# Batch 0's keys turned in pairs of tokens, in another order with scores and products, and an earlier load of batch 1's values

## The chip, the cores and the metric

The kernel runs on one core of a Trainium2 chip. A core has a matrix engine (TensorE, PE in the profile, with its weight loads as PEld), VectorE (DVE), ScalarE (ACT), GpSimd (POOL) and SyncE (SP); the last two issue most of the transfers. Matrix products land in PSUM, eight banks of 128 partitions by 2 KB. The metric is device microseconds of one execution.

## The reference

There are 4 batches, 8 heads, 768 tokens and 64 features a head. The first part is attention whose keys and values are mixed between blocks of 96 tokens by a matrix P (8 x 8 a head), made doubly stochastic by five rounds; the second is an MLP over tokens and channels.

```python
for _ in range(5):
    P = exp(P - max); P = P / sum over -1; P = P / sum over -2
k_sorted = einsum('bhij,bhjcd->bhicd', P, k_b)     # v_sorted likewise
scores = scale * q_b @ k_sb^T                      # within a block of 96
attn = softmax(scores);  x = attn @ v_sb           # -> (4, 768, 512)
u = x + lam * (w_tok @ (alpha1 * x + beta1))
out = u + lam * (relu((alpha2 * u + beta2) @ w_ch1) @ w_ch2)
```

## The kernel before

Every engine works off its instructions in the order in which the program gives them (the `Engine` wrapper pins it). The framework puts in the waits, and hands out the buffers: PSUM is cut into two slots of two banks (`psa`) and four slots of one bank (`psb`), and a tile that needs a slot waits until all readers of the one before are done. In SBUF the tag `raw` has two buffers, shared by `k8` and `v8` (keys and values of batch 0), by the permuted second half of the token weights, and by the keys and values of the later batches.

Batch 0 is done apart from the others, with an order written out by hand (lines 900 to 1013). A "group" `g` is a pair of heads; there are four. The steps that matter here:

- `v_sort`, `v_mm`, `v_out` (lines 171, 393, 408) reorder, mix and store the values of batch 0 into `Vs`.
- `k_turn(0, g, psb)` (line 387, through `turn_slab`, line 238) mixes the keys of a group and turns them so that features lie on partitions. It takes one token at a time: for each of 12 tokens and both heads the 64 x 64 piece of `k8` is the stationary operand and `bigK` the moving one. Output half `t // 6` goes to one of two psB banks, on the 64 partitions of its head. `k_copy` (line 390) copies one bank, 128 partitions of 384 elements, into `KT0`, the keys that the scores read; one bank goes to VectorE (`copy`), the other to ScalarE (`act.copy`).
- `score(0, g, hf, ps)` (line 414) makes the scores of four blocks of a group and their exponentials on ScalarE, in one piece where the slot is `psa` and in two where it is two `psb` slots. With `fillers` it runs idle matmuls first.
- `pv_first(g)` (line 464) multiplies them with `Vs` (24 matmuls or so), and VectorE divides by the sums (`rc`, `x`).
- `wtok` turns the token weights, `first_mm(g)` is the first token product, `first_turn` turns x; then the units of the channel MLP (`h_unit`, `ch_unit`) follow, with the steps of the next batch put between them by the table `at` (`put`, lines 993 to 1071).
- `prep_scales` (line 272) is two short multiplications on VectorE. `scale_weights(g)` (line 793) scales a quarter of `W2p` on VectorE.
- `load_kv(b)` (line 195) issues the loads of the values and the keys of batch b from GpSimd's queue, each in two halves; `mix_v(1, n)` and `mix_k(1, n)` use them, `q_turn_late` the queries that `load_q(1)` brings.

In the order before, the keys of groups 0 and 1 are turned among the value products, then all four scores of these groups follow, then `pv_first(0)`, then the keys of groups 2 and 3:

```python
    score(0, 0, 0, psa)
    score(0, 0, 1, psa)
    score(0, 1, 0, psb, 1)
    score(0, 1, 1, psb)
    ...
    pv_first(0)
    kp2 = k_turn(0, 2, psb)
    kp3 = k_turn(0, 3, psb)
```

GpSimd's queue issues, in this order, the weights `W1p` and `W2p` (four blocks each, with the permutation of the token weights between them), then the values and keys of batch 1 and its queries.

Of the kernel before, what the change touches and what calls it, by code (L numbers as in the profile page):

```python
# [7 lines left out]
FT = mybir.dt.float32  # L8
# [8 lines left out]
def kernel(  # L17
# [31 lines left out]
    HB = BLK // 2  # L49
# [23 lines left out]
    pe = Engine(nc.tensor)  # L73
    dve = Engine(nc.vector)
    act = Engine(nc.scalar)
# [11 lines left out]
    def psa(shape, dtype, name):  # L87
        return pools["psA"].tile(shape, dtype, name=name, tag="psA")

    def psb(shape, dtype, name):  # L90
        return pools["psB"].tile(shape, dtype, name=name, tag="psB")

    def const(shape, dtype, name):
        return wts.tile(shape, dtype, name=name, tag=name)

    wz = const([128, 512], F16, "wz")
# [13 lines left out]
    KT0 = att.tile([128, H4, NB, 128], F16, name="kT0", tag="tw", bufs=2)  # L110
# [3 lines left out]
    k8 = att.tile([128, H4, 12 * D], F16, name="k8", tag="raw", bufs=2)  # L114
# [7 lines left out]
    def load_halves(dst, src):  # L122
        for th in range(2):
            pool.dma_start(
                dst[th * 64:(th + 1) * 64, :, :],
                src.rearrange("h (j th t) d -> th (h j) t d", j=NB, th=2)[th],
            )
# [64 lines left out]
                qn_of[b][:, kt, :, :], q[b, :, kt * 128:(kt + 1) * 128, :].rearrange("h p d -> p h d"),  # L192
            )

    def load_kv(b):
        for kv, src in ((1, v), (0, k)):
            raw = att.tile([128, HB, D], F16, name="raw", tag="raw", bufs=2)
            load_halves(raw, src[b])
            raw_of[(b, kv)] = raw
# [38 lines left out]
    def turn_slab(src, rhs, g, name, ps):  # L238
        if ps is psa:
            ps = ps([128, 2, 512], FT, name)  # L240
            ps = [ps[:, a, 0:384] for a in range(2)]
        else:
            ps = [ps([128, 384], FT, name)[:] for a in range(2)]
        for s in range(12):
            for h2 in range(2):
                t = (s + 6 * h2) % 12
                r = slice(h2 * 64, h2 * 64 + 64)
                pe.matmul(
                    ps[t // 6][r, (t % 6) * 64:(t % 6) * 64 + 64],
                    src[r, g, t * D:(t + 1) * D], rhs(r, g), start=True, stop=True,  # L250
                )
        return ps
# [19 lines left out]
    def prep_scales():  # L272
        dve.tensor_tensor(
            ab2col[:, 3 * CT:4 * CT], ab2col[:, 2 * CT:3 * CT], ab2col[:, 3 * CT:4 * CT], ALU.mult
        )
        dve.tensor_tensor(ab2col[:, 4 * CT:5 * CT], ab2col[:, 0:CT], ab2col[:, 3 * CT:4 * CT], ALU.mult)
# [44 lines left out]
    bigK = {}  # L321
# [65 lines left out]
    def k_turn(b, g, ps):  # L387
        return turn_slab(k8, lambda r, g: bigK[b][r, g, :], g, "k_ps", ps)

    def k_copy(b, g, ps, half, eng):  # L390
        eng(
            KT0[:, g, :, :].rearrange("p i (th u) -> p (i th) u", th=2)[:, :, 0:HB].rearrange(
                "p x (c t) -> p x c t", t=12
            )[:, :, :, half * 6:half * 6 + 6],
            ps[half].rearrange("p (t x c) -> p x c t", t=6, c=4),
        )

    def v_mm(b, n, out_):
        for s in range(8):
            for th in range(2):  # L400
                d = (s + 4 * th) % 8
                r = slice(th * 64, th * 64 + 64)
                pe.matmul(
                    out_[r, d * 64:d * 64 + 64], VD[r, n * 8 + d, :],
                    bigV[b][r, :, :].rearrange("p h i -> p (h i)"), start=True, stop=True,
                )

    def v_out(n, w, src, eng):
        eng(Vs[:, :, n * 8:(n + w) * 8], src.rearrange("p (d x) -> p x d", x=64))
# [4 lines left out]
    def score(b, g, hf, ps, fillers=0):  # L414
        if ps is psb:
            ps = [ps([128, 4 * BLK], FT, "sc_ps") for _ in range(2)]
            bank = [t_[:] for t_ in ps]
        else:
            ps = [ps([128, 2, 512], FT, "sc_ps")]
            bank = [ps[0][:, a, :] for a in range(2)]  # L420
        for _ in range(fillers):
            z = wz[:].bitcast(FT)[:, 0:192]
            pe.matmul(
                bank[0][:, 0:384], z[:, 0:128], z.unsqueeze(1).to_broadcast([128, 2, 192]), start=True, stop=True,
            )
        n = 128 if b == 0 else BLK
        keys = kT_of[b][:].rearrange("p g i t -> p (g i t)")
        for ii in range(4):
            i = 4 * hf + ii
            lo = (g * NB + i) * n  # L430
            w = min(128, H4 * NB * n - lo)
            for h2 in range(2):
                r = slice(h2 * 64, h2 * 64 + 64)
                pe.matmul(
                    bank[h2][0:w, ii * BLK:(ii + 1) * BLK], keys[r, lo:lo + w],
                    qT_of[b][r, g, i * BLK:(i + 1) * BLK], start=True, stop=True,
                )
        tag, bufs = ("ost", 4) if (b, g) == (0, 3) else ("et", 6)
        et = att.tile([128, 2, 4, BLK], F16, name="et", tag=tag, bufs=bufs)
        if len(ps) == 1:  # L440
            act.activation(
                et[0:n].rearrange("p a i t -> p a (i t)"), ps[0][0:n, :, 0:4 * BLK], AF.Exp, scale=scale
            )
        else:
            for a in range(2):
                act.activation(
                    et[0:n, a].rearrange("p i t -> p (i t)"), ps[a][0:n, :], AF.Exp, scale=scale
                )
        ets[(b, g, hf)] = et
# [11 lines left out]
        dve.tensor_tensor(dst, x_of[b][rows, kts, c], al, ALU.mult)  # L461
        dve.tensor_tensor(dst, dst, be, ALU.add)

    def pv_first(g):
        if g == 0:
            x_of[0] = moep.tile([128, 8, C], F16, name="x128", tag="x128", bufs=1)
        ps = psa([128, 2, 512], FT, "x_ps")[:, :, 0:480].rearrange("p a (k d) -> p a k d", d=80)
        for i in range(NB):
            for h2 in range(2):
                et = ets[(0, g, i // 4)][:].rearrange("p a i t -> p (a i t)")  # L470
                lo = (4 * h2 + i % 4) * BLK
                w = min(128, 8 * BLK - lo)
                val = Vs[:, (2 * g + h2) * NB + i, 0:D + 1]
                if i < 6:
                    pe.matmul(ps[0:w, h2, i, 0:D + 1], et[:, lo:lo + w], val, start=True, stop=True)
                else:
                    for a in range(3):
                        pe.matmul(
                            ps[96:128, h2, 3 * (i - 6) + a, 0:D + 1], et[:, lo + a * 32:lo + (a + 1) * 32], val,
                            start=True, stop=True,  # L480
                        )
        rc = att.tile([128, 2, 6], FT, name="rc", tag="rc", bufs=3)
        dve.reciprocal(rc[:], ps[:, :, :, D])
        dve.tensor_tensor(
            x_of[0][:, 0:NT, g * 128:(g + 1) * 128].rearrange("p k (a d) -> p k a d", a=2),
            ps[:, :, :, 0:D].rearrange("p a k d -> p k a d"),
            rc[:].rearrange("p a k -> p k a").unsqueeze(3).to_broadcast([128, NT, 2, D]), ALU.mult,
        )
# [406 lines left out]
    copy = dve.tensor_copy  # L895
# [24 lines left out]
    v_mm(0, 5, v5)  # L920
    v_mm(0, 2, v12[:, 512:1024])
    v_out(0, 1, v0, copy)
    kp0 = k_turn(0, 0, psb)
    v_out(6, 2, v67, copy)
    v4 = bank("v_ps")
    v_mm(0, 4, v4)
    v3 = bank("v_ps")
    v_mm(0, 3, v3)
    v_out(5, 1, v5, act.copy)
    k_copy(0, 0, kp0, 0, copy)  # L930
    k_copy(0, 0, kp0, 1, act.copy)
    kp1 = k_turn(0, 1, psb)
    v_out(4, 1, v4, copy)
    v_out(1, 1, v12[:, 0:512], act.copy)
    v_out(3, 1, v3, copy)
    v_out(2, 1, v12[:, 512:1024], act.copy)
    k_copy(0, 1, kp1, 0, copy)
    k_copy(0, 1, kp1, 1, act.copy)
    score(0, 0, 0, psa)
    score(0, 0, 1, psa)  # L940
    score(0, 1, 0, psb, 1)
    score(0, 1, 1, psb)
    prep_scales()
    pool.tensor_tensor(brow[0:1, :], bet1[:], lam1[:], ALU.mult)
    for j in range(1, 4):
        sp.dma_start(brow[32 * j:32 * j + 1, :], brow[0:1, :])
# [7 lines left out]
        pool.dma_start(W1p[:, :, g * 512:(g + 1) * 512], w1v[:, :, g * 512:(g + 1) * 512])  # L954
    permute(1, pool.tensor_copy, 0, 6)
    for g in range(4):
        pool.dma_start(W2p[:, g * 4:(g + 1) * 4, :], w2v[:, g * 4:(g + 1) * 4, :])
    moe_start(0)
    a1_of[0] = moep.tile([128, 8, C], F16, name="a1", tag="a1", bufs=1)
    pv_first(0)  # L960
    kp2 = k_turn(0, 2, psb)
    kp3 = k_turn(0, 3, psb)
    for g, kp in ((2, kp2), (3, kp3)):
        k_copy(0, g, kp, 0, copy)
        k_copy(0, g, kp, 1, act.copy)
    score(0, 2, 0, psa)
    score(0, 2, 1, psb)
    pv_first(1)
    score(0, 3, 0, psb)
    score(0, 3, 1, psa)  # L970
    for ks in range(4):
        wtok(ks, copy)
    wtok(4, act.copy)
# [10 lines left out]
    first_turn(2, psa)  # L984
    scale_affine(betaB)

    load_kv(1)
    load_q(1)
    pool.memset(Vs[0:BLK, :, D:GRP], 1.0)

# [23 lines left out]
    for b in range(1, B):  # L1014
        p = b - 1
# [42 lines left out]
        put(b, 0, "h", 4, lambda b=b: moe_cross(b, 1))  # L1058
        put(b, 0, "c", 2, lambda b=b: moe_affine(b, 1))

    for g, m in enumerate((10, 11, 12, 12)):
        put(0, 0, "h", m, lambda g=g: scale_weights(g))
    for n, at_ in enumerate(((0, 1, "c", 4),) * 3 + ((0, 1, "c", 5),) * 3 + ((0, 1, "c", 6),) * 2):
        put(*at_, lambda n=n: block_weights(n))
# [68 lines left out]
```

## Time and profile before

| | |
|---|---|
| median of 3 runs | 258.17 us (256.55 to 260.22) |
| profiled execution, its own time | 256.33 us |
| its span | 254.6 us |
| TensorE busy | 244.0 us (96%), mean granted clock 0.993 |
| VectorE, ScalarE, GpSimd busy | 174.1, 155.7, 46.1 us |
| moved by DMA | 31.09 MB, mean 122 GB/s |

The profile is of one execution. Times in it count from the first instruction, and the span ends with the last. Nearly every instruction carries line 65, the line of the wrapper, so that groups are told apart by the tiles they write and read: `k_ps` are the turned keys in PSUM and `kT` the copy of them, `sc_ps` scores, `et` their exponentials, `x_ps` the attention products, `wtok_ps` token weights, `tok_ps` token products, `raw` the loads of later batches. A chain of waits follows the work that ended last backwards, from each instruction to what released it. A table of windows gives the busy time of each engine in stretches of the span, then the granted clock of TensorE, the share of the DMA engines and GB/s.

### The profile page before, as it was taken

Reading aid. Unit: us, or ns where it says so; the run is one execution under the profiler, and the core shown is the slowest. Engines: PE = TensorE matmul, PEld = TensorE weight load, DVE = VectorE, ACT = ScalarE, POOL = GpSimd, SP = SyncE. Lnnn points to the kernel's source line nnn. Section 1 sums busy time; section 2 is a strip of 40 time slices with the busy share of each in tenths; the row PEclk is TensorE's granted clock in tenths of the full one; section 3 lists DMA queues with packets and bytes.
Section 4 is the critical chain, followed back from the end, with each engine's and each line's share of the span. In section 5 each row is a group of like instructions: output and inputs, shape, how many; then the busy total and the mean of one; then the engine's idle time right before and its main releaser. Section 6 shows DMA issues by size and latency. Waiting matters only on the chain.

```text
span 254.6 us, 6059 instructions
## 1 busy us (share of the span) xinstructions
PE 244.0 (96%) x2416; PEld 159.7 (63%) x2416; DVE 174.1 (68%) x461; ACT 155.7 (61%) x285; POOL 46.1 (18%) x70
## 2 busy tenths in 40 slices
PE   7897999999999999999999999999999999999994
PEld 2475765555465545556765797558756875686783
DVE  5884588667379868279896685398978862462773
ACT  4796675567788679786564696878364005837400
POOL 8699604000082010191000010000000000000000
PEclk9997999999999999999999999999999999999999
DMA  5999999998999997999961179710203132111023
GB/s 98 202 210 192 207 205 210 216 179 197 165 179 180 131 209 124 178 159 164 136 161 39 31 189 127 141 23 0 85 0 66 50 115 45 21 41 44 0 85 82
DMA packets 61936, 31.09 MB, mean 122 GB/s; under 512 B 50562, under 2 KB 57618, under 8 KB 61908
## 3 DMA queue, kind: packets, MB, share of 16 engines
q0 software_dynamic: 20976, 16.91, 45.7%
q1 hardware_dynamic: 40836, 13.76, 32.0%
q8 instruction: 19, 0.31, 0.5%
q14 instruction: 9, 0.07, 0.1%
q10 hardware_dynamic: 96, 0.03, 0.1%
HBM read 32.79 MB, written 8.65 MB: 163 GB/s over the span
## 4 chain that ended last, share of the span: by engine, by line
PE 77%; DVE 9%; ACT 6%; DMA 3%; issue 2%; POOL 1%; DVEq 0%; ACTq 0%; POOLq 0%
PE h_ps L65 28%; PE tok_ps L65 12%; PE px L65 8%; PE ch_ps L65 8%; PE pz L65 6%; PE py L65 5%; DMA v<-in_v_dram 3%; PE x_ps L65 3%; DVE x L65 3%; PE sc_ps L65 2%; DVE sums L65 2%; PE kmix_ps L65 2%; PE mix_ps L65 2%; ACT kT L65 1%; ACT vd L65 1%
## 5 line engine op out<-in xcount | busy, mean ns | idle before, releaser
L65 PE MATMUL h_ps<-a2T,W1p 128*128 128x384 bf16 x512 | 93.4, 326 | 0.3 <-DVE a2T L65 0.3
L65 PEld LDWEIGHTS <-W1p 128*128 128x128 bf16 x512 | 47.8, 98 | 30.7
L65 ACT ACTIVATE hTa<-h_ps 128x384 f16<-128x384 f32 x64 | 31.2, 490 | 30.6 <-PE h_ps L65 29.5
L65 ACT ACTIVATE hTb<-h_ps 128x384 f16<-128x384 f32 x64 | 31.3, 489 | 8.7 <-PE h_ps L65 8.7
L65 DVE SCALAR_TENSOR_TENSOR u<-tok_ps,x 128x512 f32<-128x512 f32 x21 | 14.5, 692 | 27.0 <-PE tok_ps L65 27.0
L65 PE MATMUL tok_ps<-a,w_tokT 128*128 128x512 f16 x126 | 30.3, 379 | 0.0
L65 ACT CAST kT<-kmix_ps 64x512 f16<-64x512 f32 x36 | 25.7, 713 | 7.0 <-PE kmix_ps L65 6.5
L65 ACT ACTIVATE et<-sc_ps 96x768 f16<-96x768 f32 (+2 forms) x36 | 24.6, 736 | 2.4 <-PE sc_ps L65 2.4
L65 ACT CAST u<-u 128x512 f16<-128x512 f32 x21 | 13.0, 618 | 20.4 <-DVE u L65 20.4
L65 PEld LDWEIGHTS <-sums 128*128 128x128 f16 x216 | 21.1, 98 | 3.8 <-issue 0.7
L65 PEld LDWEIGHTS <-hTa 128*128 128x128 f16 x192 | 18.2, 98 | 6.6
L65 PEld LDWEIGHTS <-hTb 128*128 128x128 f16 x200 | 18.5, 98 | 6.1
L65 PEld LDWEIGHTS <-w_tokT 128*128 128x128 f16 x126 | 12.3, 98 | 13.1 <-DVE a L65 0.3
L65 DVE TENSOR_TENSOR x<-x_ps,rcb 96x512 f16<-96x512 f32 x24 | 16.5, 687 | 0.8
L65 DVE TENSOR_TENSOR sums<-hTa,hTb 128x512 f16<-128x512 f16 (+2 forms) x27 | 8.9, 330 | 10.3 <-ACT hTb L65 10.0
L65 PEld LDWEIGHTS <-et 96*128 96x128 f16 (+4 forms) x288 | 12.6, 103 | 2.7
L65 DVE SCALAR_TENSOR_TENSOR ost<-px,u 128x256 f32<-128x256 f32 x27 | 11.3, 419 | 3.4 <-PE px L65 3.4
L65 PE MATMUL x_ps<-Vs,et 96*128 96x65 f16 (+4 forms) x288 | 13.5, 199 | 0.0
L65 PE MATMUL ch_ps<-W2p,hTa 128*128 128x512 f16 x48 | 11.9, 380 | 0.0
L65 PE MATMUL ch_ps<-W2p,hTb 128*128 128x512 f16 x48 | 11.7, 379 | 0.0
L65 POOL DMA_DIRECT2D qn<-in_q_dram x12 | 10.7, 915 | 5.2 <-DMA raw<-in_v_dram 4.8
L65 PE MATMUL sc_ps<-qT,kT 64*128 64x96 f16 (+1 forms) x256 | 10.0, 210 | 1.5 <-DVE x L65 0.7
(140 smaller groups left out, 351.2 us busy)
## 6 DMA issues: line engine op xcount, KB each, us to landing
out_dram<-ost SPq DMA_DIRECT2D x23, 192.0 KB, 2.4
raw<-in_v_dram POOLq DMA_DIRECT2D x6, 384.0 KB, 8.4
raw<-in_k_dram POOLq DMA_DIRECT2D x6, 384.0 KB, 10.8
Vs<-vscr SPq DMA_DIRECT2D x3, 768.0 KB, 7.9
W1p<-in_moe_w_ch_dram POOLq DMA_DIRECT2D x4, 512.0 KB, 11.6
W2p<-in_moe_w_ch_dram POOLq DMA_DIRECT2D x4, 512.0 KB, 15.6
qn<-in_q_dram POOLq DMA_DIRECT2D x12, 128.0 KB, 11.1
vscr<-mixed POOLq DMA_DIRECT2D x4, 384.0 KB, 5.0
```

The costliest lines, as they stand in the source:

```text
L65: ins = getattr(self.eng, name)(*args, **kwargs)
```

## The change

The keys of batch 0 are turned two tokens at a time: a 64 x 128 piece of `k8` is stationary, 12 matmuls a group in place of 24, and a head has a bank of its own, with the even tokens on its lower 64 partitions and the odd ones on the upper. A bank is copied in two pieces of 64 partitions, which write every second token. The keys of group 2 are now turned ahead of `pv_first(0)`, the scores of group 1 and the keys of group 3 follow behind it; `pv_first(0)` starts with one idle matmul; both banks of group 3 are copied by VectorE; some scores change between `psa` and `psb`; `prep_scales` comes later. The values of batch 1 are issued ahead of the last block of `W2p`, and the scaling of that block moves from unit 12 to unit 15 of the first half.

```diff
-    def load_kv(b):
-        for kv, src in ((1, v), (0, k)):
+    def load_kv(b, *kvs):
+        for kv in kvs or (1, 0):
+            src = (k, v)[kv]
...
+    def k_turn_pairs(g):
+        ps = [psb([128, 384], FT, "k_ps")[:] for a in range(2)]
+        for tp in range(6):
+            for h2 in range(2):
+                r = slice(h2 * 64, h2 * 64 + 64)
+                pe.matmul(
+                    ps[h2][:, tp * 64:tp * 64 + 64], k8[r, g, tp * 128:(tp + 1) * 128], bigK[0][r, g, :],
+                    start=True, stop=True,
+                )
+        return ps
+
+    def k_copy_pairs(g, ps, h2, eng):
+        dst = KT0[h2 * 64:h2 * 64 + 64, g, :, :].rearrange("p i (th u) -> p (i th) u", th=2)[:, :, 0:HB].rearrange(
+            "p x (c t) -> p x c t", t=12
+        )
+        for par in range(2):
+            eng(
+                dst[:, :, :, par::2],
+                ps[h2][par * 64:par * 64 + 64, :].rearrange("p (t x c) -> p x c t", t=6, c=4),
+            )
...
-    def pv_first(g):
+    def pv_first(g, fillers=0):
...
+        z = wz[:].bitcast(FT)[:, 0:240]
+        for _ in range(fillers):
+            pe.matmul(ps[:, 0, :], z[:, 0:128], z.unsqueeze(1).to_broadcast([128, 2, 240]), start=True, stop=True)
...
-    kp0 = k_turn(0, 0, psb)
+    kp0 = k_turn_pairs(0)
...
-    k_copy(0, 0, kp0, 0, copy)
-    k_copy(0, 0, kp0, 1, act.copy)
-    kp1 = k_turn(0, 1, psb)
+    k_copy_pairs(0, kp0, 0, copy)
+    k_copy_pairs(0, kp0, 1, act.copy)
+    kp1 = k_turn_pairs(1)
...
-    k_copy(0, 1, kp1, 0, copy)
-    k_copy(0, 1, kp1, 1, act.copy)
     score(0, 0, 0, psa)
     score(0, 0, 1, psa)
-    score(0, 1, 0, psb, 1)
-    score(0, 1, 1, psb)
-    prep_scales()
+    k_copy_pairs(1, kp1, 0, copy)
+    k_copy_pairs(1, kp1, 1, act.copy)
+    kp2 = k_turn_pairs(2)
+    k_copy_pairs(2, kp2, 0, copy)
...
     for g in range(4):
+        if g == 3:
+            load_kv(1, 1)
         pool.dma_start(W2p[:, g * 4:(g + 1) * 4, :], w2v[:, g * 4:(g + 1) * 4, :])
...
-    pv_first(0)
-    kp2 = k_turn(0, 2, psb)
-    kp3 = k_turn(0, 3, psb)
-    for g, kp in ((2, kp2), (3, kp3)):
-        k_copy(0, g, kp, 0, copy)
-        k_copy(0, g, kp, 1, act.copy)
+    pv_first(0, 1)
+    score(0, 1, 0, psa)
+    k_copy_pairs(2, kp2, 1, act.copy)
+    kp3 = k_turn_pairs(3)
+    k_copy_pairs(3, kp3, 0, copy)
+    k_copy_pairs(3, kp3, 1, copy)
+    prep_scales()
+    score(0, 1, 1, psb)
     score(0, 2, 0, psa)
-    score(0, 2, 1, psb)
+    score(0, 2, 1, psa)
     pv_first(1)
-    score(0, 3, 0, psb)
-    score(0, 3, 1, psa)
+    score(0, 3, 0, psa)
+    score(0, 3, 1, psb)
...
-    load_kv(1)
+    load_kv(1, 0)
...
-    for g, m in enumerate((10, 11, 12, 12)):
+    for g, m in enumerate((10, 11, 12, 15)):
         put(0, 0, "h", m, lambda g=g: scale_weights(g))
```

More of the change, by code (lines that the diff above doesn't have):

```diff
@@ L462, in first_affine @@
         dve.tensor_tensor(dst, dst, be, ALU.add)
-    def pv_first(g):
+    def pv_first(g, fillers=0):
         if g == 0:
             x_of[0] = moep.tile([128, 8, C], F16, name="x128", tag="x128", bufs=1)
-        ps = psa([128, 2, 512], FT, "x_ps")[:, :, 0:480].rearrange("p a (k d) -> p a k d", d=80)
+        ps = psa([128, 2, 512], FT, "x_ps")[:, :, 0:480]
+        z = wz[:].bitcast(FT)[:, 0:240]
+        for _ in range(fillers):
+            pe.matmul(ps[:, 0, :], z[:, 0:128], z.unsqueeze(1).to_broadcast([128, 2, 240]), start=True, stop=True)
+        ps = ps.rearrange("p a (k d) -> p a k d", d=80)
         for i in range(NB):
```

## The prediction

> **What bounds the kernel now.** I read the page's engine line and the 40 slices first, then the chain of waits in its early part, then a table of windows, the rows of the key copies, and the transfers.
>
> ```profile
> PE 244.0 (96%) x2416; PEld 159.7 (63%) x2416; DVE 174.1 (68%) x461; ACT 155.7 (61%) x285; POOL 46.1 (18%) x70
> ...
> PE   7897999999999999999999999999999999999994
> ...
> PEclk9997999999999999999999999999999999999999
> DMA  5999999998999997999961179710203132111023
> ```
>
> From slice 5 on (each is 6.4 us) TensorE is never below nine tenths: from about 41 us it only works off its list, so what the front loses or gains there is passed on to the end one for one. The DMA line says that the transfers fill the engines until about 58 us. So there are two things to follow: the front on the engines, and the arrivals. The chain of waits in the front:
>
> ```profile
> 16.96 0.39 ACT kT L65
> 17.35 2.96 ACT et L65 x6
> 20.31 0.91 issue
> 21.22 0.59 PE k_ps L65 x23
> 21.81 0.02 issue
> 21.83 0.57 DVE kT L65
> 22.40 0.14 issue
> 22.54 0.63 PE sc_ps L65 x16
> 23.16 1.57 PE x_ps L65 x24
> ```
>
> ScalarE is the bound up to 20.3 us, from 12 us on by the same chain (value copies, key copies, six exponentials of the scores of groups 0 and 1). Then TensorE, which had begun the keys of group 2 at 19.53, stands until 21.22: their psB banks are held by the scores of group 1. That wait is 1.48 us long in the list of waits. What it leaves behind is seen in windows cut to the clock's own steps:
>
> ```profile
> 15.97:19.39 3.42, 3.34 (x90) 2.41 (x83) 2.17 (x6) 3.42 (x9) 3.02 (x6) 1.00 1.16 211
> 19.39:22.80 3.41, 1.56 (x68) 1.31 (x66) 2.16 (x4) 1.77 (x5) 3.41 (x4) 1.00 1.20 165
> 22.80:26.21 3.41, 3.41 (x60) 2.94 (x54) 1.46 (x4) 2.59 (x6) 3.41 (x5) 0.50 1.16 220
> ```
>
> The second number is TensorE's busy time and the third from the right its granted clock. After a window with 1.56 us of work in 3.41 us (46%) the clock is half for the next one; the emptiest window before it that was not followed by this had 83%. In the half window the 24 products of `pv_first(1)` take 1.64 us, against 1.02 us for `pv_first(0)`.
>
> **The change, part by part.** The times below are of the span of the profiled execution (254.6 us; its own time is 256.33 us).
>
> *The turn.* 96 matmuls become 48. 24 of them took 0.55 us; sixteen score products, the nearest form with 64 rows and 128 columns, took 0.51 to 0.59 us, so twelve should take some 0.4 us. That is 0.1 to 0.2 us a group, on an engine that waits for banks and copies here. I take nothing; with no wait left it would be a gain of at most 0.8 us. One page of the Trainium skill speaks against it: "TensorEngine Tiling (Array Packing)", section "Tiling Modes", says that changing the tiling mode drains the engine, and the value products (64 by 64) now alternate with key turns of 64 by 128. Here a key turn of 64 by 64 runs from 16.03 to 16.84 us and the 64 by 128 scores behind it start at 16.77, inside it, so I count no drain; by the rule it would be one matmul's 0.19 us at each of some three added switches.
>
> *The copies.* Each bank now needs two copies of 64 partitions in place of one of 128. Four copies on VectorE become ten, four on ScalarE become six. The rows:
>
> ```profile
> L65 ACT CAST kT<-k_ps x4: 477/482/483, 15.5 to 22.2; 128x384 f16<-128x384 f32 x4
> L65 DVE CAST kT<-k_ps x4: 548/548/559, 15.7 to 22.3; 128x384 f16<-128x384 f32 x4
> ...
> 57.48 1.42 ACT L65 CAST kT<-kmix_ps 64x512 f16<-64x512 f32 x2 [2.45 <-PE kmix_ps L65]
> ```
>
> Back to back what counts is the distance of starts: 0.37 us on ScalarE (15.50 to 15.87) and 0.47 us on VectorE. The new copy is not in the trace. Low end on ScalarE: 0.37 us, as for 128 partitions. High end: 0.71 us, that of the later batches' key copies, two of which take 1.42 us. These also take 64 partitions and write every second element, but move 512 elements; by 384/512 that is 0.53 us, and I take it as the nearest in form. On VectorE I take 0.47, with 0.67 us (the same ratio of 0.53 to 0.37) as the high end.
>
> *The new order on ScalarE.* Starts: keys of group 0 at 15.50; value copies at 16.56 and 17.04 (0.48 each); exponentials of group 0 at 17.52 and 18.22 (0.70 each, 17.25 to 17.95 before); keys of group 1 at 18.92 and 19.45, done at 20.05. TensorE: `pv_first(0)` gets its psA slot when the first exponential is done (18.34), runs the added filler (two of 384 columns took 0.91 us, so about 0.5 us for 480) and 24 products in 1.02 us: about 19.9 us against 19.60. Only now come the scores (0,1,0), at 20.1, because the keys of group 1 end on ScalarE at 20.05; their exponential starts at 20.5. Then the second bank of group 2's keys, 21.2 to 22.3. The scores (0,1,1) want psB banks, and one of the four is held until that copy ends (or until VectorE's copies of group 3 at about 22.2): they start at 22.35. So the wait of 1.48 us isn't removed; TensorE stands from about 20.85 (end of the turn of group 3) to 22.35, 1.5 us, now behind key copies on ScalarE. Queued behind it on TensorE are (0,2,0), (0,2,1) and `pv_first(1)`, and ScalarE idles 0.5 us at each of two round trips. Exponentials of (0,1,1) 22.75 to 23.5, of (0,2,0) to 24.2, of (0,2,1) to 24.9. `pv_first(1)` needs the psA slot of (0,2,0), free at 24.3, because both scores of group 2 now sit in psA: it runs from 24.35 to 25.37 us at full clock, to 25.99 at half. Before it ended at 24.73.
>
> *To the first token product.* VectorE then does the reciprocal and the division (0.27 and 0.92 us) and five token-weight copies (1.47 us, 25.95 to 27.43), and the last matmul of `first_mm(0)` adds about 0.35: 25.37 + 0.03 + 0.27 + 0.92 + 1.47 + 0.35 = 28.4 us at full clock, 29.0 at half. Before it ended at 28.09. So the front loses 0.3 or 0.9 us. TensorE's work in 19.39 to 22.80 by this order is about 1.6 us of 3.41, near the 1.56 that was followed by the half clock, but where the windows fall differs from run to run. I take +0.5. Bounds: three pairs of key copies lie on this path, so 0.37 gives 3 x 2 x 0.16 = 0.96 less (-0.7) and 0.71 gives 1.08 more (+1.4 at full, +2.0 at half clock). The slower VectorE copy is hidden: group 3 would end at 23.9, and its scores start past 25.
>
> The Trainium skill, "TensorE: Matmul & The Clock Gate", section "Why this matters for your kernels", puts the drop of the clock at idle gaps of some 3 us. This trace differs: the longest gap before the half clock is 1.5 us. By the page no half clock would come here and the loss would be 0.3.
>
> *Small moves.* `prep_scales` (0.35 us on VectorE) goes from 17.83 to about 23.1, where VectorE has nothing until 25.4; its first reader is at 28.12 on ScalarE. `scale_weights(3)` (1.22 us) goes from unit 12 to unit 15, but is VectorE work that ran at 53.87 anyway, for matmuls at about 56. Both nothing.
>
> *The values of batch 1.*
>
> ```profile
> 25.72 2.96 POOL L65 DMA_DIRECT2D W2p<-in_moe_w_ch_dram  x4
> 28.95 0.54 POOL L65 DMA_DIRECT2D raw<-in_v_dram  x1 [0.26 <-PE x_ps L65]
> 31.21 0.53 POOL L65 DMA_DIRECT2D raw<-in_v_dram  x1 [1.72 <-DMA W1p<-in_moe_w_ch_dram]
> ```
>
> The second half is issued at 31.21 and lands 18.7 us later, at 49.9; the first `mix_v` starts at 50.78, so 0.9 us are to spare. The queue works in order and 512 KB take about 2.5 us, so with the last W2p block behind it the values land at 47.4 and that block at 49.9, where it is wanted at 53.87. W2p's last issue moves behind GpSimd's wait at 29 to 31 us (an issue waits until the eighth before it has landed: W1p's second block, 19.17 + 11.8 = 31.0). Behind it stand only the keys of batch 1, which waited until 40.76 anyway. The buffer that the values need is k8's, free after the turn of group 3 (20.85), and GpSimd comes there at 27.9. In the profiled execution this is worth nothing. In the median run it may be: that is 1.84 us longer than the profiled one. If late transfers are the whole of it, they are 2.74 us late; the next arrivals have 2.5 us (queries, 41.77 + 13.9 = 55.7 against 58.23) and 3.3 us (keys, 53.6 against 56.83), so 0.2 us is paid in place of 1.84: a gain of 1.6. If none of it is, zero. I take 0.8.
>
> **Sum.** 258.17 + 0.5 - 0.8 = 257.9; against the profiled execution's 256.33 it is +0.5, 256.8.
>
> **Rivals.** (1) *The front gets shorter.* The new copy costs ScalarE 0.37 and the clock stays full: -0.7. For it: half as many elements in all per copy. Against it: the later batches' copies. With the 0.8 of the loads 256.7, with 1.6 255.9; I give 256.3. (2) *Slower: the new wait on ScalarE.* The copy costs 0.71, TensorE stands 2 us before (0,1,1), and the half clock falls on `pv_first(1)`: +2.0, and no gain of the loads: 260.2. It decides as soon as a pair of copies takes over 1.2 us and the work in that window is near 46%. For it: all these copies sit on the engine that bounds the front. (3) *The earlier load isn't earlier*, because its buffer or its queue place isn't free: +0.5 and no gain, 258.7; the times 20.85 and 27.9 speak against it.
>
> **How the numbers follow.** Forecast 0.50 (its own range 256.3 to 259.2), rival 1 0.22, rival 2 0.20, rival 3 0.08. 255.9 and 260.2 are the ends of the unknown costs; as the runs of before lie from 256.55 to 260.22 about their median, I add about 1 below and 0.6 above: 254.8 to 260.8. 2% of the median, about what a measurement of this kernel can tell from no change, is 5.2 us. No case reaches that by itself: faster needs under 253.0, rival 1 and lucky runs (0.09); slower over 263.3, rival 2 and unlucky ones (0.08).
>
> **What would show it.** Right: the key copies of 64 partitions on ScalarE about 0.53 us apart; TensorE idle about 1.5 us ahead of the scores (0,1,1), released by ScalarE's kT; `first_mm(0)` done between 28.2 and 29.0; the values of batch 1 landed by 48 us; the slices after 41 us alike. Wrong: `pv_first(1)` done before 24.7, `first_mm(0)` before 27.8, a wait at `mix_v` or ahead of the last W2p block, or a time outside 254.8 to 260.8.

## The result and the profile after

The changed kernel takes 261.0 us (median of 6 runs, 260.66 to 262.30); the kernel before took 257.44 beside it (6 runs, 256.55 to 260.22): a loss of 3.6 us, where 257.9 us was forecast. The ratio on record is 1.0166 with a 95% interval of 1.0134 to 1.0199 (the two medians alone would give 1.0138). Two later sets of runs with the same kernel gave 259.63 (1.0098, 1.0054 to 1.0141) and 261.20 (1.0147, 1.0098 to 1.0195); single executions lie from 259.1 to 262.4, with one at 264.2. So the loss is 2 to 3.6 us by the medians, slower in each of the three intervals, but inside the 2% that counts as no change here.

The profiled execution took 262.3 us, its span 260.5. Its engine line, TensorE's slices and the granted clock:

```profile
PE 247.5 (95%) x2368; PEld 161.3 (62%) x2368; DVE 177.4 (68%) x467; ACT 157.8 (61%) x285; POOL 46.1 (18%) x70
...
PE   7966799999999999999999999999999999999994
...
PEclk9997589999999999999999999999999999999999
```

Slices 3 to 5 (13 to 33 us) have got emptier, slices 5 and 6 slower; from slice 7 on the digits are those of before. The chain of waits of the same execution, in the front:

```profile
20.02 3.19 PE x_ps L65 x26
...
24.50 0.57 ACT kT L65
...
25.72 0.35 PE sc_ps L65 x7
26.07 1.57 ACT et L65 x3
...
27.69 1.61 PE x_ps L65 x24
29.30 0.45 PE sc_ps L65 x8
...
29.78 1.20 ACT et L65 x2
...
31.02 1.44 PE wtok_ps L65 x12
32.46 1.77 PE tok_ps L65 x6
```

Before, one run of exponentials led to one run of TensorE. Now TensorE and ScalarE take turns: two idle and 24 real products (26 in the first row), scores, key copy, scores, exponentials, `pv_first(1)`, scores, exponentials, and only then the last token weights. `first_mm(0)` ends at 34.23 in place of 28.09.

Not all of these 6.1 us need belong to the change. The first value copies on ScalarE start at 11.99 in the profile of before and at 13.35 here, and between 11.9 and 13.7 in all profiles, whatever the kernel (13.31 with the loads alone, e4 below). The changed kernel's third profile (run e18 below, the fastest of its six executions) starts them at 11.93, so it stands beside before without that shift: `first_mm(0)` ends at 30.78 and the span is 257.3, both 2.7 us more than before. The rest of the span after `first_mm(0)` is 226.5 us in before, 226.3 here and 226.5 there. In these profiles the whole loss is in the front, and it is passed on one for one.

### The profile page after: what moved, and what is told of

Read it like the earlier page. It is cut to its first block, busy times and chain, and to the rows that moved or that the text cites. A ratio compares the mean times of both kernels' runs of the same rounds, so it can differ in the third digit from the quotient of the medians.

```text
span 260.5 us, 5966 instructions
## 1 busy us (share of the span) xinstructions
PE 247.5 (95%) x2368; PEld 161.3 (62%) x2368; DVE 177.4 (68%) x467; ACT 157.8 (61%) x285; POOL 46.1 (18%) x70
## 4 chain that ended last, share of the span: by engine, by line
PE 83%; ACT 7%; DVE 5%; DMA 2%; issue 1%; DVEq 0%; POOLq 0%
PE h_ps L65 30%; PE tok_ps L65 12%; PE px L65 8%; PE ch_ps L65 7%; PE pz L65 6%; PE py L65 5%; PE x_ps L65 4%; PE sc_ps L65 3%; ACT kT L65 2%; DMA q<-in_q_dram 2%; PE q_ps L65 2%; ACT et L65 2%; PE warm_ps L65 2%; PE kmix_ps L65 2%; PE mix_ps L65 1%; DVE x L65 1%
## 5 line engine op out<-in xcount | busy, mean ns | idle before, releaser
L65 PEld LDWEIGHTS <-et 96*128 96x128 f16 (+4 forms) x288 | 13.4, 106 | 5.1 <-issue 2.5
L65 PE MATMUL x_ps<-Vs,et 96*128 96x65 f16 (+4 forms) x288 | 14.1, 203 | 1.3 <-ACT et L65 1.3
L65 PEld LDWEIGHTS <-kT 64*128 64x128 f16 (+1 forms) x256 | 6.7, 98 | 9.1 <-issue 5.8
L65 PE MATMUL ch_ps<-W2p,hTa 128*128 128x512 f16 x48 | 11.9, 380 | 0.0
```

The lines of the kernel that those rows point to most:

```text
L65: ins = getattr(self.eng, name)(*args, **kwargs)
```

## The experiments

The theory after the first profile: the new order replaces one wait by a series of turns between TensorE and ScalarE, which cost time themselves; the idle matmul, the dearer key copies and the half clock add to it. The rivals: the copies alone, the half clock alone, the idle matmul alone.

**The three parts alone.** e1 has only the pairs, e2 only the order (with the idle matmul and the moved loads), e4 only the loads; e3 is the changed kernel without the idle matmul.

```diff
# e1_pairs_old_order, on the kernel before (all four groups)
-    kp0 = k_turn(0, 0, psb)
+    kp0 = k_turn_pairs(0)
-    k_copy(0, 0, kp0, 0, copy)
+    k_copy_pairs(0, kp0, 0, copy)
...
# e2_new_order_single, on the changed kernel (all four groups)
-    kp0 = k_turn_pairs(0)
+    kp0 = k_turn(0, 0, psb)
...
# e3_no_filler, on the changed kernel
-    pv_first(0, 1)
+    pv_first(0)
# e4_load_only, on the kernel before
     for g in range(4):
+        if g == 3:
+            load_kv(1, 1)
...
-    load_kv(1)
+    load_kv(1, 0)
...
-    for g, m in enumerate((10, 11, 12, 12)):
+    for g, m in enumerate((10, 11, 12, 15)):
```

> The kernel before with the turn of two tokens at a time and its doubled copies, all in the order before. Theory A (the new order empties TensorE while it waits for key copies and slots, and the half clock that follows is what costs): the order is the old one, so at most 1 us over before, from copies that take about 0.58 us each on ScalarE: 257.4 to 258.5 us, one half-clock window as before. Theory B (the doubled copies cost by themselves, because ScalarE is the bound here): six more copies' worth, about 2.5 to 3.5 us over before: 260 to 261. Theory C (the earlier load of the values): no change, 257.4.

> The changed kernel with its order, its idle matmul and its loads, but with keys turned one token at a time and one copy of 128 partitions a bank. Theory A: the waits for key copies and slots stay, a little shorter, and the half clock with them: 259.5 to 261. Theory B: the loss is gone: 257 to 258. Theory C: 261.

> The changed kernel without the idle matmul ahead of the first attention product. Theory A with the idle matmul as part of the harm (it took 1.7 us at the half clock and the first attention product waited behind it): 259.5 to 260.3, about 1 us less than the changed kernel. Theory A with the idle matmul as a protection of the clock: 261 to 262. Theories B and C: 260.5 to 261, no change.

> The kernel before with only the earlier load of batch 1's values and the later scaling of the last block of the second weight. Theories A and B: as before, 257.4, or up to 0.8 us less where the values came late. Theory C (the moved transfers cost): 259 to 261, with a wait ahead of the products of that block or of the values.

| | us | ratio to before (95%) |
|---|---|---|
| e1, pairs in the old order | 258.54 | 1.0037 (1.0009 to 1.0065) |
| e2, new order, one token | 259.94 | 1.0098 (1.0068 to 1.0128) |
| e3, changed without the idle matmul | 259.36 | 1.0056 (1.0020 to 1.0092) |
| e4, loads alone | 257.26 | 0.9988 (0.9947 to 1.0028) |

Each part but the loads costs something. By their times e1, within 0.1 us, and e2 come out where theory A put them; e3 lies 0.14 us below its range. The price of the copies is read from the rows of the key copies, here of the changed kernel (count; shortest, median and longest in ns; first and last start):

```profile
L65 DVE CAST kT<-k_ps x10: 559/580/591, 16.8 to 26.2; 64x384 f16<-64x384 f32 x10
L65 ACT CAST kT<-k_ps x6: 572/575/584, 17.0 to 25.1; 64x384 f16<-64x384 f32 x6
```

Two in a row start 0.58 us apart on ScalarE: with 64 partitions the distance is the whole duration, while the copies of 128 partitions came 0.37 apart at 0.48 each.

**The order without the idle matmul, and the waits filled.** e5 is e2 without the idle matmul; e6 is e3 with idle matmuls put ahead of three waits, so that the clock stays full; e7 puts six idle matmuls where TensorE waits in the kernel before, and e12 takes the idle matmul of before away.

```diff
# e5_order_alone, on e2
-    pv_first(0, 1)
+    pv_first(0)
# e6_stalls_filled, on e3: ahead of k_turn_pairs(1), score(0, 1, 1), pv_first(1)
+    warm(3)
...
+    warm(7, psb)
...
+    warm(5, psb)
# e7_before_filled, on the kernel before, behind pv_first(0)
+    warm(6)
# e12_before_no_filler, on the kernel before
-    score(0, 1, 0, psb, 1)
+    score(0, 1, 0, psb)
```

> The changed kernel's order and loads with keys one token at a time, one copy a bank, and no idle matmul: the order alone. If the parts of the loss add up (whole 1.66%, idle matmul about 1.1%, doubled copies 0.4 to 0.7%), the order alone is within 0.4% of before: 257.2 to 258.4 us. Rival: the waits of the new order (for the exponential ahead of the second product, 1.3 us in the changed kernel) cost by themselves and the idle matmul only shifts where TensorE stands: 259.3 to 260.

> The changed kernel with its idle matmul taken out and idle matmuls put where TensorE stands anyway, in PSUM slots that are free there: 3 of 512 columns ahead of the turn of group 1, 7 ahead of the second scores of group 1, 5 ahead of the second attention product. If the half clock is what makes the waits dear: granted clock 0.993 or more, 258.0 to 258.7 us, 0.7 to 1.3 us less than without them (259.4). If the waits themselves are the whole loss: 259.2 to 259.7, and over 260 if the fillers delay what stands behind them.

> The kernel before with six idle matmuls of 512 columns behind the first attention product, where TensorE stands 1.3 to 1.5 us for the scores' banks. Clock theory: the half-clock window at 23 to 26 us falls away: granted clock 1.0, 0.6 to 1.3 us less than before, ratio 0.995 to 0.998. Rival (the half clock falls on work that waits for ScalarE and VectorE anyway): ratio 0.999 to 1.002.

> The kernel before without its idle matmul ahead of the scores (0,1,0). If idle matmuls there cost as much as the one in the changed kernel: 0.5 to 1 us less than before. If ScalarE's exponentials hide it, as the profile before has it (they run without a gap from 17.25 to 20.3): no change, 257.0 to 257.8, or more where the clock falls earlier.

e5 took 259.27 us (1.0071, 1.0039 to 1.0103), e6 259.44 (1.0065, 1.0030 to 1.0101), e7 258.01 (1.0004, 0.9970 to 1.0037), e12 257.59 (1.0009, 0.9979 to 1.0040). The table of windows cut to the clock's steps (second number TensorE's busy time, third from the right its clock), first the changed kernel, then e6:

```profile
20.30:23.71 3.41, 3.41 (x44) 2.15 (x45) 1.71 (x5) 1.56 (x4) 3.41 (x4) 0.50 1.17 178
23.71:27.13 3.42, 0.90 (x34) 0.71 (x29) 3.30 (x7) 3.00 (x6) 3.42 (x5) 1.00 1.19 216
27.13:30.54 3.41, 2.85 (x46) 2.52 (x46) 1.18 (x4) 1.97 (x4) 2.19 (x4) 0.50 1.24 208
30.54:33.95 3.41, 3.20 (x21) 2.19 (x20) 1.70 (x6) 1.29 (x4) 0.78 (x1) 0.50 1.24 206
```

```profile
20.41:23.82 3.41, 2.85 (x52) 1.66 (x51) 3.29 (x7) 2.54 (x5) 3.27 (x4) 1.00 1.16 174
23.82:27.23 3.41, 3.20 (x58) 2.09 (x52) 3.28 (x5) 2.74 (x5) 3.41 (x5) 1.00 1.21 204
```

The changed kernel has three half-clock windows where before had one; e6 has none, and in time it equals e3 (259.44 and 259.36). The half clock is thus not the sole cause: with the clock full, `first_mm(0)` still ends at 29.73 in e6, against 28.09 before. But the equal times don't show that the idle matmuls only pay for themselves. In e3's profile `first_mm(0)` ends at 31.56, so the front of e6 is 1.8 us shorter. Of this 1.3 us are lost again later, most of it at one wait that e3's profile doesn't have, for a step of VectorE that itself waits 2.1 us for a transfer (`uT`):

```profile
103.47 0.61 PE L65 MATMUL h_ps<-a2T,W1p 128*128 128x384 bf16 x2 [0.87 <-DVE a2T L65]
```

From the end of `first_mm(0)` the span has another 227.6 us in e6, 228.7 in e12 (1.49 us of the same wait), 227.7 in e2 and 227.1 in e7, where before and the changed kernel have 226.3 to 226.5. So a gain in the front isn't always passed on. Why that transfer comes too late in these profiles stays open.

e7 and e12 also say what most of the wait of before was. In each line of TensorE's timeline below the bracket gives the length of the stop ahead of it and its releaser: e7, e12 and e5.

```profile
20.94 1.25 PE L65 MATMUL warm_ps<-wz 128*128 128x512 f16 x5 [1.10 <-issue]
```

```profile
20.91 0.91 PE L65 MATMUL k_ps<-bigK,k 64*64 64x64 f16 x45 [1.04 <-issue]
```

```profile
21.34 0.31 PE L65 MATMUL x_ps<-Vs,et 128*32 128x65 f16 x5 [1.55 <-issue]
```

No semaphore releases these. In before, e4, e5, e7 and e12 the stop stands behind exactly 705 records of TensorE (weight loads, matmuls, semaphores), whatever comes next: a key turn, an idle matmul, a product in the middle of `pv_first(0)`. For before and e4 the profile names ScalarE's exponentials, but these had ended 0.91 and 0.72 us earlier. The kernels with pairs, which issue fewer instructions, do not show the stop, nor does e2. In e5 it falls ahead of the scores of group 1, which may be why the order alone loses as much as order and pairs together.

The obvious guess is that the next instructions weren't there yet, and the traces bear it out. The profile lists DMA queues that it calls "instruction"; one of them (q8) moves packets of 16 KB. In the five kernels TensorE goes on 1.41 to 1.52 us after the end of such a packet (19.5 to 20.9 us). e7 has a second stop 256 records further on, at 28.04, 1.54 us after the end of the next packet; the profile names a copy of VectorE for it, which had ended 0.52 us earlier. The other kernels come to their 705th record later, in e2 1.29 us and in the kernels with pairs 2.2 us or more after the packet, and none stops there. No run changed the packets, so this is an argument and not a test.

e7 keeps the clock full and its ratio is its rival's, but its six idle matmuls run behind the stop, so that the keys of group 2 start at 22.20 in place of 21.22: it is no clean test of the half clock.

**The copies made cheaper or moved.** e8 and e11 are e1, and e10 is e9, with copies that write six neighbouring tokens instead of every second one. e8 leaves out the matching order of the values, so that tokens within a block are permuted; e10 and e11 reorder the values too, and e11 has no idle matmul. e9 is e3 with the second bank of group 2 copied by VectorE at once.

```diff
# e8, e10, e11 (e10 and e11 with v_sort writing the same order)
-                dst[:, :, :, par::2],
+                dst[:, :, :, par * 6:par * 6 + 6],
# e9_copy_moved, on e3
     k_copy_pairs(2, kp2, 0, copy)
+    k_copy_pairs(2, kp2, 1, copy)
...
-    k_copy_pairs(2, kp2, 1, act.copy)
```

> The kernel before with the turn in pairs, where each copy of 64 partitions writes six neighbouring tokens in place of every second one (this leaves out the right order of the tokens within a head). One look at the distance of two copies of one bank. If the strided writes make them dear: 0.37 us on ScalarE and 0.47 us on VectorE, as for the copies of before. If it is the 64 partitions or the shift between partitions: 0.58 and 0.60 us as with the strided writes.

> The changed kernel without its idle matmul, and with the second bank of group 2's keys copied by VectorE, ahead of the first attention product, in place of ScalarE behind the exponential of (0,1,0). Theory W (the loss is the waits of the new order themselves, above all TensorE's 1.8 us for ScalarE's key copy, which holds a psB bank): that wait goes, 258.0 to 258.5 us, about 1 us less than the 259.4 without the idle matmul. Rival P (the two psA slots bound it: the second product waits for the exponentials of group 2 wherever the copies are): 259.1 to 259.6.

> As the run before, and the copies write six neighbouring tokens: within each run of 12 tokens the even ones come first, in the keys and by the reordering of the values as well, so the result is the same. Copies 0.48 us apart on ScalarE in place of 0.58. Theory W: four copies on ScalarE lie on the path, 0.3 to 0.5 us less than the run before. Rival P: no difference. If the reordering of the values gets slower by its pattern, the values end later than 3.1 us after they begin and the time is over the run before.

> The order before with the turn in pairs, neighbouring writes as in the run above, and without the idle matmuls that the scores of group 1 begin with (they took 1.5 us at the half clock in a run with pairs). TensorE has 96 records fewer and so no stop at its 705th record. If that stop and the idle matmuls were what cost there: 256.0 to 257.0, a little under before. If the doubled copies decide: 257.5 to 258.5.

In e8 ScalarE's copies are cheaper, VectorE's hardly (540 to 559 ns):

```profile
L65 ACT CAST kT<-k_ps x8: 472/474/475, 15.6 to 23.6; 64x384 f16<-64x384 f32 x8
```

They start 0.49 us apart, so of the 0.21 us by which a pair member is dearer than a copy of before (0.58 against 0.37) some 0.09 is the strided write and 0.12 the lost overlap. In time that buys nothing that can be told: e8 257.53 (one execution), e11 258.78 (1.0047, 1.0013 to 1.0081, without one execution of 962.4 us) against e1's 1.0037, e10 258.69 (1.0041, 0.9998 to 1.0084) against e9's 258.16 (1.0044, 1.0013 to 1.0075). e11 was to take 256.0 to 257.0 if the stop and the idle matmuls were what cost; it is far from that.

**The steps side by side.** The changed kernel, e3, e9 and e1 once more, in one set of runs.

> The changed kernel once more, in one call with the three steps that lead to it, so that the loss can be split. Theory (the losses add up): 1.017 of before, 260.9 to 261.8 us, of which the idle matmul is about 1.6 us. Rival (the parts were measured on different runs of before and the split is chance): the ratio moves by more than 0.004 from 1.0166.

> The changed kernel without the idle matmul. Theory: 1.5 to 2 us below the changed kernel of the same call, 1.006 to 1.009 of before. Rival (the idle matmul only fills time in which TensorE would wait for the group-1 keys anyway): within 0.5 us of the changed kernel.

> Without the idle matmul, and with the second bank of group 2's keys copied on VectorE at once rather than later on ScalarE. Theory (the waits on ScalarE's key copy are a cost of their own): the ScalarE wait ahead of the scores (0,1,1) is gone and the time is 0.6 to 1.2 us below the one before it, 1.002 to 1.005 of before. Rival (the wait is only moved to the first product of group 1): no more than 0.3 us less.

> Keys turned two tokens at a time in the order of before. Theory (the copies of 64 partitions cost what they measured, about 0.1 to 0.2 us more each, with some four of them on the path): 1.003 to 1.006 of before. Rival (nothing of the loss is in the copies): 1.000 to 1.002.

| | us | ratio to before (95%) |
|---|---|---|
| e13, the changed kernel | 259.63 | 1.0098 (1.0054 to 1.0141) |
| e14, without the idle matmul | 259.29 | 1.0065 (1.0034 to 1.0096) |
| e15, and the copy on VectorE | 258.71 | 1.0040 (1.0009 to 1.0071) |
| e16, pairs in the old order | 258.72 | 1.0040 (1.0006 to 1.0075) |

The ratios of e1, e3 and e9 repeat within 0.1%; that of the changed kernel moves by 0.0068, which is e13's rival: the split by the earlier runs was in part chance. By the medians the moved copy is worth 0.6 us here and 1.2 by the earlier runs, the idle matmul 0.3 here (within the 0.5 of e14's rival) and 1.6 there; by the ratios it is 0.6 and 0.3 for the copy, 0.9 and 2.8 for the idle matmul. The intervals of neighbours overlap: the order of the steps came out the same both times, their sizes are not firm. What the moved copy does is plain in e15's timeline: the scores (0,1,1) now wait 0.38 us, on VectorE, where the changed kernel waits 1.78 on ScalarE, and the products of `pv_first(1)` 0.33 where it waits 1.30 (a wait of 0.43 for VectorE's division is new between them).

```profile
21.67 0.82 PE L65 MATMUL sc_ps<-qT,kT 64*128 64x96 f16 x15 [0.38 <-DVE kT L65]
...
23.76 1.62 PE L65 MATMUL x_ps<-Vs,et 128*128 128x65 f16 x24 [0.33 <-ACT et L65]
```

**The idle matmul by dose.** Six passes in place of two, beside the changed kernel on the same chip.

```diff
# e17_filler_tripled, on the changed kernel (e18 is the changed kernel)
-    pv_first(0, 1)
+    pv_first(0, 3)
```

> The changed kernel with six passes of the idle matmul ahead of the first attention product in place of two. One pass took 0.53 us at full clock and 0.87 at half in the profiles so far. Theory (the idle matmul is paid in full, because the scores of group 1 and their exponentials wait behind it): four more passes, 2.1 to 3.5 us over the changed kernel of the same call. Rival (it only fills time in which TensorE waits anyway, and what it does is keep the clock): under 1 us.

> The changed kernel, on the same chip as the tripled idle matmul. So far 261.0 us (1.0166 of before) in one set of runs and 259.6 (1.0098) in another. Theory (two kinds of executions, by where the half-clock windows fall): single times from 259.2 to 262.5, the median between the two. Rival (a difference of the chips): all of them near one of the two.

e17 took 261.78 us (1.0148, 1.0102 to 1.0193), e18 261.20: 0.6 us for four more passes, under the theory's 2.1 and within the rival's 1. The two profiles start at the same time and show why. TensorE's timeline, e17 first:

```profile
18.68 2.68 PE L65 MATMUL x_ps<-wz 128*128 128x480 f32 x6
...
26.53 1.00 PE L65 MATMUL x_ps<-Vs,et 128*128 128x65 f16 x24 [1.30 <-ACT et L65]
```

```profile
18.58 1.07 PE L65 MATMUL x_ps<-wz 128*128 128x480 f32 x2
...
24.87 1.61 PE L65 MATMUL x_ps<-Vs,et 128*128 128x65 f16 x24 [0.98 <-ACT et L65]
...
28.20 1.44 PE L65 MATMUL wtok_ps<-ident,wp 128*128 128x128 f16 x12 [0.21 <-ACT et L65]
29.43 1.35 PE L65 MATMUL tok_ps<-w_tokT,x 128*128 128x384 f16 x6
```

The four passes are paid in full up to `pv_first(1)`, 1.66 us later (0.41 each); the theory had this right. But the half clock then begins only at 27.65 in place of 23.04, `pv_first(1)` takes 1.00 in place of 1.61, and at the end of `first_mm(0)` 1.07 us of the 1.66 are left. So neither view holds alone: idle products delay everything behind them and may buy a faster clock a few microseconds on. e18's six executions spread from 259.07 to 262.42, the range that its theory of two kinds gave, but without clear groups, so that two kinds aren't shown.

No kernel here beats the kernel before: e4, e7 and e12 equal it within their intervals.

## Why the prediction was wrong

Its steps against e18, the profile that starts when before's did and the fastest of its executions (before's time in brackets):

| step | predicted | measured |
|---|---|---|
| key copies of 64 partitions, ScalarE / VectorE | 0.53 / 0.47 | 0.58 / 0.57 to 0.61 |
| products of `pv_first(0)` begin (18.58) | 18.8 | 19.49 |
| TensorE's wait ahead of the scores (0,1,1) | 1.5 on ScalarE's kT | 1.89, 1.78 in the first profile |
| `pv_first(1)` begins (23.09) | 24.35 | 24.87 |
| `pv_first(1)` ends (24.73) | 25.37, at half clock 25.99 | 26.48 |
| from there to the end of `first_mm(0)` (3.36) | 3.04 | 4.30 |
| end of `first_mm(0)` (28.09) | 28.4, at half clock 29.0 | 30.78 |

**What held.** The front of the changed kernel passes its loss on one for one. TensorE's wait ahead of the scores (0,1,1), released by ScalarE's key copy, and that of `pv_first(1)` for a psA slot were both named, with near sizes. The copies lie within their bounds. The turn in pairs brings no gain in time.

**What was misread, without much effect.** The wait of 1.48 us in before did not end with the psB banks: 0.91 us of it come after the last exponential, at the 705th record, and the changed kernel doesn't have that stop. What it has is a new wait of about the same length; that "the wait isn't removed" gave the right size is luck. And there is a price for changes of tiling, though a small one. By the starts of single matmuls, the first key turn follows the 64 by 64 value products after 0.03 us in before, where both have the same tiling, and after 0.12 in e18, where it is 64 by 128; the way back takes 0.12 too. Ends are modelled, so the overlap that the prediction went by couldn't show this. It is 0.1 us a change, half of the 0.19 that the prediction named for each of some three added changes.

**The step that failed: the way from `pv_first(1)` to `first_mm(0)`.** The prediction put it on VectorE, as a division and five token-weight copies back to back, 3.04 us at either clock. That is below the 3.36 us that before itself took, and the chain of before, by its rows the bound, had it on TensorE: 0.76 of scores, 1.53 of token weights, 1.07 of token products. Matmuls take longer at half clock (the 24 products of `pv_first(1)` 1.61 us in e18, 1.00 in e17), and in the new order the last token weights also wait for the exponentials of group 3. With the clock full the way takes 3.48 us (e6), with the half clock until 27.83 us 3.63 (e9), until 29.86 4.30 (e18), until 30.82 4.75 (e13), until 33.95 4.93 (the first profile). The forecast counted the half clock only on `pv_first(1)`. It missed 1.3 us here, in the first profile 1.9; of the 1.3 some 0.4 are there at full clock, by e6, and by these runs the rest goes with the half clock.

**The idle matmul** was put at 0.5 us, from a row in which "two of 384 columns" took 0.91. That row's `x2` are the two passes of one idle matmul (`score` issues one there), so 0.91 was the price of one. Here, too, one matmul runs in two passes. They delay the products by 0.91 us in e18, and by 1.52 (20.02 to 21.54) in the first profile, where they fall into a half-clock window. That misses 0.4 to 1.0, which would account for most of the 0.5 us by which `pv_first(1)` begins late in e18.

**The half clock.** The page "TensorE: Matmul & The Clock Gate" of the Trainium skill, section "Why this matters for your kernels", ties the drop to idle gaps of some 3 us. The runs differ: e18's window from 19.62 to 23.04 is 45% busy, its longest gap is 1.89 us, and half clock follows. But the 46% that the prediction read from one row is no threshold either: half clock followed windows 58%, 59% and 71% busy (e10, e12, e8), and in e17 a window with 55% is not followed by it, while the next one with 52% is:

```profile
20.82:24.23 3.41, 1.88 (x47) 1.33 (x46) 1.94 (x4) 1.68 (x3) 3.41 (x5) 1.00 1.15 171
24.23:27.65 3.42, 1.78 (x56) 1.62 (x57) 1.88 (x6) 2.56 (x5) 3.42 (x6) 1.00 1.23 210
27.65:31.06 3.41, 3.20 (x37) 2.55 (x32) 2.68 (x7) 2.06 (x4) 1.11 (x3) 0.50 1.24 207
```

**The loads.** The values are issued at 28.22 and 29.09 and land at 47.7 us in the first profile, at 48.1 in e18, where 47.4 was predicted; the products that use them start past 53 in both. The 0.8 us taken for it rested on the guess that late transfers made the median longer than the profiled execution. e4 shows no effect that can be told, 0.9988 (0.9947 to 1.0028), though a gain of 0.8 us would lie within that interval. The spread may be in part that of the start of the value copies.

**The sum with the measured terms.** +0.5 becomes +2.7 (28.09 to 30.78), and -0.8 becomes 0 by e4: 258.17 + 2.7 = 260.9, against 261.0. That this agrees so closely is luck: against the 257.44 measured beside it 0.9 of the 3.6 us is left, which the first profile of the changed kernel, with more half clock, could hold. So the forecast fell out of its range by sizes that all erred one way. The second rival (260.2) had the right place, ScalarE's copies and the half clock on `pv_first(1)`, and nearly the wait (2 us), but the wrong price, 0.71 for a copy.

**Open.** How the loss divides between the idle matmul (0.3 to 2.8 us, by what is compared), the late copy (0.3 to 1.2) and the half clock, since each shifts the windows of the clock; and why the changed kernel's median differs by up to 1.6 us from one set of runs to another.

## What to carry to other kernels

Follow the chain of waits to the stage from which time is passed on, and take a stage's price from the chain's own rows: a sum below what the kernel before takes for the same stage is a warning. Where two engines take turns, each change of turn can cost a wait, even where every wait seems moved rather than added. A gain in the front is sure only when the later waits for transfers are looked at too. Price every matmul on such a path at both clocks, idle ones too: they are paid at once and may be repaid later by the clock. And ask what a row counts before its price is taken: two records can be one matmul.

## What was not expected of the hardware

TensorE stopped for 1.0 to 1.6 us behind its 705th record in five kernels, with no semaphore to release it, and went on 1.41 to 1.52 us after a 16 KB packet of the queue called "instruction" had ended; 0.91 us of "issue" in the chain of before was this, and idle matmuls put there don't fill it. A change of tiling costs about 0.1 us (starts 0.12 us apart in place of 0.03). ScalarE copies of 64 partitions don't overlap one another (0.58 us apart at 0.58 each, those of 128 partitions 0.37 apart at 0.48), and writing neighbouring elements in place of every second takes 0.1 us off ScalarE's copy and about 0.02 off VectorE's. The value copies begin between 11.9 and 13.7 us, from one execution to the next. In e11's execution of 962.4 us the 512 products of `h_ps` took 951 ns each in place of 326, with a granted clock of 1.000 in the record; the cause is not known.
